# A new order for the work items of a recurrent-attention kernel, with three small moves in its feed-forward part and its head

## The chip, the cores and the metric

One core of one Trainium2 chip runs the whole kernel. The metric is device time in microseconds (us) of one execution; for each kernel the median of several runs is compared. The core has five engines with an instruction queue each: TensorE for matmuls (PE in the profile, PEld for its weight loads), VectorE (DVE), ScalarE (ACT), GpSimd (POOL), and SyncE (SP), which in this kernel only issues DMAs. The 16 DMA engines of the core move data between device memory (dram tensors) and the on-chip memory (`arena` in the profile). Matmul results land in eight banks of `ps`. An engine works through its own queue in order; waits on semaphores tie the queues together.

## The reference

The output is `g * a + (1 - g) * b` with three parts computed from the same x (2048 tokens of 640 values), all in bf16.

```python
def _A_ref(x, mem0, Wq, Wk, Wv, Wo, seg_len):      # 64 segments of 32 tokens, 32 heads of 192
    mem = mem0                                     # 8 rows
    for s in range(n_seg):
        h = concatenate([mem, x[s*32:(s+1)*32]])   # 40 rows of 640
        q, k, v = h @ Wq, h @ Wk, h @ Wv           # per head
        p = softmax(where(mask, q @ k.T * Dh**-0.5, -1e9))
        o = (p @ v) @ Wo
        mem = o[:8]; outs.append(o[8:])
    return concatenate(outs)
def _B_ref(x, w_gate, w_up, w_down):               # 640 -> 1536 -> 640
    return (gelu(x @ w_gate) * (x @ w_up)) @ w_down
g = sigmoid((x * gate_w).sum(-1, keepdims=True))
return g * a + (1 - g) * b
```

The mask of the reference is `(idx[:, None] < M) | (idx[:, None] >= idx[None, :])`. What matters for the time is the recurrence: the first eight rows of a segment's result are the memory of the next segment, so the 64 segments run one after the other. The projections of the 32 tokens that are no memory do not depend on it.

## The kernel before, in words

**Queues and dependencies.** The kernel writes one list of operations. A small scheduler class (`_Sched`) puts each operation at the end of its engine's queue, in the order in which the Python code emits it, and works out from the memory regions that it reads and writes which semaphores it waits for. Nothing is reordered later. Of several waits of a PE operation some are put onto the last matmuls of the operation before it. SP's queue is in program order too.

**Stages.** First the feed-forward part B for all tokens, in four blocks of 512 tokens: five transposed tiles of x (`ffn_transposes`, L818, on DVE), then for each of 12 tiles f the matmuls G (L828) and U (L831, five matmuls each), the gelu on ACT (L834) and the product h on DVE (L836); then `ffn_down`, which for each of four groups a of 128 tokens sums 12 tiles f, two matmuls a tile (512 and 128 columns: L850, L853). A few warming matmuls (L811) stand ahead. The result goes to a dram tensor, `ffn_b_scratch`.

Then come the four "left units" (L919), ahead of segment 0. The kernel calls "left" the tokens of a segment that it gathers over a group of four segments, because the eight-row memory and 24 of the 32 tokens fill a matmul's 32 rows, and eight tokens a segment are left over: eight tokens of four segments make another set of 32 rows. A left unit projects Q and K of one octet (one of four sets of eight heads) for such a group: matmuls, rows copied by ACT (L924), transposed by DVE (L926), stored to `left_qk_scratch`, from which a segment loads what it needs. Left V is projected apart (`vl_mm`, then `vl_evac`, which copies the bank on DVE or ACT).

Then come the 64 segments. `segment(s)` walks a list written out by hand, `PROGS[s % 4]`: the list `PROG` for s % 4 of 0, 1 and 2 and the list `PROG3` for 3. Each item makes the operations of one piece of work at the place where it stands in the list:

- `g n k`: piece k (of five along the 640) of the projections of group n; `GROUPS` gives which of Q, K, V (0, 1, 2) of which octet are in the group (L1119, or L226 where the rows in PE's weights are kept from the matmul before). With the last k, ACT empties the banks (rows L1140; V L1143). In a segment with s % 4 of 0, the V groups also project left V.
- `tq i`, `tk i`: DVE transposes the rows of Q or K of octet i (L1154); POOL makes a padded copy for Q (L1157).
- `sc i`: the scores of an octet: the mask first (L1165), then eight and more small matmuls (L1173, L234, L1180); DVE takes the maximum and subtracts (L1192, L1194).
- `ex i`: the softmax: ACT (L1204), then four operations on DVE (L1206 to L1211).
- `pt i`: transposes of the probabilities on PE (L1227, L1232), emptied by ACT (L1245).
- `pv i`: probabilities times V (L1260, L1262), emptied by ACT (L1278).
- `wo i h`: half an octet of the last product with Wo (L1296; the last octet L1321; with s % 4 of 3 L1339 for both token sets at once).
- `lf q u k`: only with s % 4 equal to q: piece k of a left unit for a later group (eight matmuls). `le q u m`: its row copy (L924), transpose (L926) and store; for `le 1 0` the two stores go out through SP (L1374), for the others one store through ACT's queue.
- `vb k`: only with s % 4 of 3: piece k of left V for the next group.

The octets are walked 0 to 3 in even and 3 to 0 in odd segments. The weights do not all fit on the chip: octets 0 and 3 share their slots for 13 of 15 projection pieces (384 KB each) and for three Wo pieces (480 KB each). After an item has read such a slot, SP loads the other octet's piece into it (`load_piece`, L628), so that each segment loads its missing pieces while it runs. The first three Wo pieces to be used give up their slots after `wo 0 0` (two) and `wo 0 1` (one), and the three pieces that come in, W13, W14 and W15 in the order of their use, are needed by `wo 3 0` and `wo 3 1`, the last items. SP's queue also holds the loads of x (L736), of left Q and K (L970) and of B's rows (L982, L988) and the stores of the result (L993, L1036).

At the end of a segment the sums of Wo are taken from the banks and transposed (`Tm`, L1517) into the memory rows of the next segment's h, which its first projections wait for.

Of the kernel before, what the change touches and what calls it, by code (L numbers as in the profile page):

```python
# [3 lines left out]
ACTF = mybir.ActivationFunctionType  # L4
# [234 lines left out]
def _build(nc, A_x, A_mem0, A_Wq, A_Wk, A_Wv, A_Wo, seg_len, w_gate, w_up, w_down,  # L239
# [277 lines left out]
    def piece_view(key, o):  # L517
        if key[0] == 3:
# [4 lines left out]
    PROG = [("g", 0, 0), ("g", 0, 1), ("g", 0, 2), ("g", 0, 3), ("g", 0, 4), ("tq", 0), ("g", 1, 0), ("g", 1, 1),  # L523
# [12 lines left out]
    PROG3 = [("g", 0, 0), ("g", 0, 1), ("g", 0, 2), ("g", 0, 3), ("g", 0, 4), ("g", 1, 0), ("tq", 0), ("tk", 0),  # L536
# [56 lines left out]
    o = 0  # L593
# [503 lines left out]
    def proj(s, item):  # L1097
        ms = GROUPS[item[1]]
        k = item[2]
        if k == 0:  # L1100
            for mi in ms:
                bk_of[mi] = LB if s % 4 == 0 and item[1] == 2 and mi[0] == 0 else misc_bank(s, item[1])
                if mi[0] == 2 and s % 4 == 0 and (s == 0 or mi[1]):
                    bk_of[(3, mi[1])] = OB if mi[1] == 1 else LB
# [504 lines left out]
```

## Time and profile before

| what | us |
|---|---|
| median of 3 runs | 1730.37 |
| lowest and highest run | 1717.53, 1730.9 |
| profiled execution | 1724.01 |
| its span (first to last instruction) | 1722.3 |
| PE busy | 1587.5 (92%) |
| DVE busy | 1003.5 (58%) |
| ACT busy | 776.6 (45%) |
| POOL busy | 548.6 (32%) |

The span holds some 171 us of feed-forward work, then six us of left units, then the segments at some 24 us each. The profile is of one execution. In its rows, `out<-in` names the tiles that an instruction writes and reads, `L1119` is a line of the kernel, `x8` a count. A timeline row has start, length, engine, line, operation, shapes and count, and in brackets the idle time of that engine just before and what ended it. A row of waits has the waiting and the awaited work, then microseconds in total, times, and the longest. "issue" is idle time for which no semaphore is found. SPq is the issuing of DMAs by SP.

### The profile page before, as it was taken

How to read it: one execution, taken by the hardware profiler on the slowest of the kernel's cores; microseconds unless marked ns; L12 is line 12 of the kernel's file. 1: busy time of each engine (PE TensorE's matmuls, PEld its weight loads, DVE VectorE, ACT ScalarE, POOL GpSimd, SP SyncE). 2: the span in 40 equal slices, each digit the busy share in tenths (PEclk: the TensorE clock that was granted, in tenths of full speed). 3: DMA queues.
4: the chain of work that ended last, by engine and by line, in shares of the span. 5: the costliest groups of instructions: out<-in, count | busy, mean ns of one | idle time of the engine just before them, and what ended most of it. 6: DMA issues, size and time to landing. Idle time of an engine off the chain costs nothing.

```text
span 1722.3 us, 75547 instructions
## 1 busy us (share of the span) xinstructions
PE 1587.5 (92%) x37107; PEld 778.1 (45%) x28147; DVE 1003.5 (58%) x2976; ACT 776.6 (45%) x1825; POOL 548.6 (32%) x1609
## 2 busy tenths in 40 slices
PE   9999899999999999999999899999999999999986
PEld 4444345444444444454444444454544444444443
DVE  5552666566565665655656656566665656555653
ACT  2222454545454454445444444445444544445442
POOL 1100233233333233333333333333333332333332
PEclk9999999999999999999999999999999999999998
DMA  9915988988888898879888898888888888988884
GB/s 298 326 37 153 342 311 296 322 308 297 297 299 319 307 323 281 305 276 329 295 287 302 294 333 281 283 288 319 310 298 288 296 316 289 310 280 303 314 313 170
DMA packets 278102, 499.27 MB, mean 290 GB/s; under 512 B 113951, under 2 KB 139015, under 8 KB 277767
## 3 DMA queue, kind: packets, MB, share of 16 engines
q1 hardware_dynamic: 249928, 482.45, 81.0%
q10 hardware_dynamic: 27839, 11.99, 2.5%
q8 instruction: 255, 4.18, 1.0%
q14 instruction: 80, 0.66, 0.1%
HBM read 473.25 MB, written 21.09 MB: 287 GB/s over the span
## 4 chain that ended last, share of the span: by engine, by line
PE 73%; DMA 12%; DVE 6%; ACT 4%; issue 3%; POOL 1%; SPq 0%; POOLq 0%; DVEq 0%; ACTq 0%
PE ps L1119 20%; PE ps L226 18%; DMA arena<-in_A_Wo_dram 6%; PE ps L1339 6%; PE ps L1296 5%; PE ps L1260 3%; PE ps L831 3%; PE ps L828 3%; PE ps L1165 3%; DMA arena<-in_A_Wv_dram 3%; PE ps L850 2%; PE ps L919 2%; PE ps L1173 1%; DMA arena<-in_A_Wk_dram 1%; ACT arena L1143 1%
## 5 line engine op out<-in xcount | busy, mean ns | idle before, releaser
L1119 PE MATMUL ps<-arena 128*32 128x384 bf16 x8660 | 650.9, 329 | 57.7 <-DVE arena L1517 47.4
L226 PE MATMUL ps<-arena 128*32 128x384 bf16 x8960 | 651.4, 326 | 7.7 <-DVE arena L1086 1.1
L1119 PEld LDWEIGHTS ps<-arena 128*32 128x32 bf16 x8660 | 221.7, 96 | 422.2 <-issue 265.6
L1154 DVE STREAM_TRANSPOSE arena<-arena 128x384 bf16<-128x384 bf16 x512 | 274.6, 561 | 125.8 <-ACT arena L1140 124.8
L1140 ACT ACTIVATE arena<-ps 128x384 bf16<-128x384 f32 x512 | 230.3, 493 | 233.8 <-PE ps L1119 223.3
L1296 PE MATMUL ps<-arena 128*32 128x320 bf16 x3456 | 187.1, 299 | 14.7 <-issue 13.4
L1157 POOL COPY arena<-arena 64x160 bf16<-64x160 bf16 x256 | 81.3, 318 | 374.3 <-DVE arena L1154 366.7
L1278 ACT ACTIVATE arena<-ps 128x480 bf16<-128x480 f32 (+1 forms) x256 | 137.6, 537 | 119.3 <-PE ps L1262 116.4
L1192 DVE TENSOR_REDUCE arena<-ps 104x4 f32<-104x160 f32 x256 | 82.9, 324 | 162.7 <-PE ps L1180 162.7
L1143 ACT ACTIVATE arena<-ps 128x384 bf16<-128x384 f32 x256 | 124.8, 488 | 106.9 <-PE ps L1119 105.3
L1245 ACT ACTIVATE arena<-ps 128x448 bf16<-128x448 f32 x192 | 104.6, 545 | 125.8 <-PE ps L1232 125.8
L1204 ACT ACTIVATE ps<-ps 104x160 f32<-104x160 f32 x256 | 75.8, 296 | 139.0 <-DVE ps L1194 137.1
L1206 DVE TENSOR_REDUCE arena<-ps 104x4 f32<-104x160 f32 x256 | 82.4, 322 | 95.7 <-ACT ps L1204 94.6
L976 POOL COPY arena<-arena 128x96 bf16<-128x96 bf16 x256 | 71.4, 279 | 201.2 <-PE ps L1180 163.8
L1296 PEld LDWEIGHTS ps<-arena 128*32 128x32 bf16 x3456 | 97.4, 96 | 68.2 <-issue 26.2
L1339 PE MATMUL ps<-arena 128*64 128x320 bf16 x1536 | 124.6, 305 | 1.2 <-ACT arena L1278 0.9
L1286 POOL COPY arena<-arena 128x96 bf16<-128x96 bf16 x192 | 51.3, 267 | 228.8 <-ACT arena L1278 222.6
L1260 PE MATMUL ps<-arena 128*64 128x160 bf16 x1536 | 118.3, 240 | 3.4 <-issue 3.3
L919 PE MATMUL ps<-arena 128*32 128x384 bf16 x1280 | 110.4, 328 | 0.0
L1262 PE MATMUL ps<-arena 128*64 128x64 bf16 x1536 | 104.2, 193 | 1.6 <-issue 1.3
L1260 PEld LDWEIGHTS ps<-arena 128*64 128x64 bf16 x1536 | 81.5, 109 | 47.5 <-ACT arena L1143 19.7
L1339 PEld LDWEIGHTS ps<-arena 128*64 128x64 bf16 x1536 | 79.9, 111 | 34.2 <-issue 10.4
(100 smaller groups left out, 2320.6 us busy)
## 6 DMA issues: line engine op xcount, KB each, us to landing
arena<-in_A_Wk_dram SPq DMA_DIRECT2D x335, 384.0 KB, 6.6
arena<-in_A_Wv_dram SPq DMA_DIRECT2D x335, 384.0 KB, 8.6
arena<-in_A_Wo_dram SPq DMA_DIRECT2D x205, 480.0 KB, 5.6
arena<-in_A_Wq_dram SPq DMA_DIRECT2D x209, 384.0 KB, 5.0
arena<-left_qk_scratch SPq DMA_DIRECT2D x126, 96.0 KB, 5.0
left_qk_scratch<-arena ACTq DMA_DIRECT2D x45, 192.0 KB, 4.1
left_qk_scratch<-arena SPq DMA_DIRECT2D x30, 96.0 KB, 4.5
ffn_b_scratch<-arena ACTq DMA_DIRECT2D x16, 160.0 KB, 3.1
```

The lines of the kernel that those rows point to most:

```text
L226: return e.add_instruction(mybir.InstMatmult(name=nm, start_tensor_calc=like["start"], stop_tensor_calc=stop, tile_size=(128, 32), tile_po ...
L919: fns.append(lambda e, outp=outp, rhs=rhs, j=j: e.matmul(outp, lhs, rhs, start=(k == 0), stop=(k == KT - 1), tile_position=(0, 32 * j)))
L1119: fns.append(lambda e, outp=outp, rhs=rhs, j=j: e.matmul(outp, lhs, rhs, start=(k == 0), stop=(k == KT - 1), tile_position=(0, 32 * j)))
L1140: S_.add("act", lambda e, m=m, bk=bk: e.activation(out=rows_sb[m], in_=ps[:, bk, 0:384], func=ACTF.Copy), reads=[r_ps[bk]], writes=[r_rows ...
L1143: S_.add("act", lambda e, i=i, bk=bk: e.activation(out=v_sb[i % NVB].rearrange("p (c n) -> p c n", c=3), in_=ps[:, bk, 0:384].rearrange("p ...
L1154: S_.add("dve", lambda e: e.transpose(out=dst[:, :, 0:L], in_=rows_sb[m].rearrange("p (c r) -> p c r", r=L)), reads=[r_rows[m]], writes=[r ...
L1245: S_.add("act", lambda e: e.activation(out=PT, in_=ps[:, bank, 0:PTW + 128], func=ACTF.Copy), reads=[r_ps[bank]], writes=[r_PT], name="pT ...
L1260: return [lambda e: e.matmul(full, v[:, e0:e0 + 64], PTm[:, i], start=True, stop=False, tile_position=(0, 64 * i), skip_group_check=True), ...
L1262: lambda e: e.matmul(part, vl[:, e0:e0 + 64], PTl[:, i], start=False, stop=True, tile_position=(0, 64 * i), skip_group_check=True)]
L1278: S_.add("act", lambda e: e.activation(out=apx(u[:, 0, 0, :], [[rs, na], [3 * rs, 4], [1, R]]), in_=ps[:, A, 0:na * W].rearrange("p (c t r ...
L1296: fns.append(lambda e, i=i, t=t, j=j, gv=gv: e.matmul(ps[32 * j:32 * j + 32, bank, 0:2 * DJ].rearrange("p (h n) -> p h n", h=2), lhs2[i], ...
L1339: S_.add("pe", [lambda e, i=i, g_=g_, c=c, p=p: e.matmul(ps[64 * i:64 * i + 64, LB, 0:2 * DJ], U3[:, p % 4, c, :], g_[:, c, 2 * DJ * i:2 * ...
```

## The change

Four edits, made together:

- **a.** `PROG` and `PROG3` get a new order. They hold the same items. Among the moves in `PROG`: `tk 0` stands ahead of `tq 0`; `sc 0` stands behind the last piece of group 1; `le 1 0` moves ahead of `wo 0 0`, with `ex 2` between its two halves; `wo 0 0` moves behind `g 4 3`, `g 4 4` and `g 5 0`; `wo 0 1` moves behind `g 5 2` and `sc 3`; `pv 2` no longer follows `sc 3` directly; `lf 1 1 3` moves from ahead of `wo 0 1` to behind `pv 3`.
- **b.** The first G tile of the first feed-forward block is made as five operations of one matmul, each of which reads one transposed tile of x.
- **c.** In `ffn_down`, for the first group a, the 22 matmuls of the first 11 tiles of h become an operation of their own; the last two matmuls are an operation that reads all of h, as before.
- **d.** Left V of the first octet of segment 0 is projected right behind the third of the four left units and emptied by ACT; before, its pieces stood among the pieces of segment 0's second V group, and DVE emptied them. The two functions for it are defined further up.

```diff
-    PROG = [("g", 0, 0), ("g", 0, 1), ("g", 0, 2), ("g", 0, 3), ("g", 0, 4), ("tq", 0), ("g", 1, 0), ("g", 1, 1),
-            ("tk", 0), ("g", 1, 2), ("sc", 0), ("g", 1, 3), ("ex", 0), ("g", 1, 4), ("g", 2, 0), ("g", 2, 1),
-            ("g", 2, 2), ("lf", 1, 0, 0), ("pt", 0), ("tq", 1), ("tk", 1), ("sc", 1), ("g", 2, 3), ("g", 2, 4),
-            ("tq", 2), ("ex", 1), ("lf", 2, 1, 0), ("lf", 1, 0, 1), ("lf", 1, 0, 2), ("pv", 0), ("g", 3, 0),
-            ("tk", 2), ("g", 3, 1), ("g", 3, 2), ("g", 3, 3), ("pt", 1), ("lf", 2, 1, 1), ("g", 3, 4), ("sc", 2),
-            ("ex", 2), ("lf", 2, 1, 2), ("pv", 1), ("g", 4, 0), ("g", 4, 1), ("lf", 0, 1, 0), ("g", 4, 2),
-            ("lf", 1, 0, 3), ("lf", 1, 0, 4), ("lf", 1, 1, 0), ("lf", 2, 1, 3), ("lf", 1, 1, 1), ("le", 1, 0, 0),
-            ("wo", 0, 0), ("tq", 3), ("g", 4, 3), ("le", 1, 0, 1), ("g", 4, 4), ("g", 5, 0), ("g", 5, 1),
-            ("lf", 1, 1, 2), ("lf", 0, 1, 1), ("pt", 2), ("lf", 1, 1, 3), ("wo", 0, 1), ("tk", 3), ("sc", 3),
-            ("pv", 2), ("g", 5, 2), ("wo", 1, 0), ("ex", 3), ("g", 5, 3), ("wo", 1, 1), ("g", 5, 4), ("wo", 2, 0),
-            ("pt", 3), ("lf", 0, 1, 2), ("wo", 2, 1), ("pv", 3), ("lf", 1, 1, 4), ("lf", 0, 1, 3), ("lf", 0, 1, 4),
-            ("le", 0, 1, 0), ("lf", 2, 1, 4), ("le", 2, 1, 0), ("le", 0, 1, 1), ("le", 1, 1, 0), ("le", 1, 1, 1),
-            ("wo", 3, 0), ("le", 2, 1, 1), ("wo", 3, 1)]
+    PROG = [("g", 0, 0), ("g", 0, 1), ("g", 0, 2), ("lf", 2, 1, 0), ("g", 0, 3), ("g", 0, 4), ("g", 1, 0), ("tk", 0),
+            ("g", 1, 1), ("tq", 0), ("g", 1, 2), ("g", 1, 3), ("g", 1, 4), ("sc", 0), ("g", 2, 0), ("lf", 2, 1, 1),
+            ("tq", 1), ("g", 2, 1), ("tk", 1), ("g", 2, 2), ("g", 2, 3), ("ex", 0), ("g", 2, 4), ("sc", 1),
+            ("pt", 0), ("ex", 1), ("tq", 2), ("g", 3, 0), ("g", 3, 1), ("g", 3, 2), ("pv", 0), ("lf", 1, 0, 0),
+            ("lf", 1, 0, 1), ("tk", 2), ("g", 3, 3), ("lf", 2, 1, 2), ("pt", 1), ("lf", 2, 1, 3), ("lf", 0, 1, 0),
+            ("g", 3, 4), ("lf", 1, 0, 2), ("sc", 2), ("pv", 1), ("lf", 1, 0, 3), ("lf", 1, 0, 4), ("lf", 0, 1, 1),
+            ("g", 4, 0), ("g", 4, 1), ("lf", 2, 1, 4), ("tq", 3), ("le", 1, 0, 0), ("ex", 2), ("g", 4, 2),
+            ("le", 1, 0, 1), ("lf", 1, 1, 0), ("g", 4, 3), ("g", 4, 4), ("lf", 1, 1, 1), ("g", 5, 0), ("wo", 0, 0),
+            ("tk", 3), ("g", 5, 1), ("pt", 2), ("lf", 1, 1, 2), ("g", 5, 2), ("sc", 3), ("lf", 0, 1, 2),
+            ("wo", 0, 1), ("wo", 1, 0), ("ex", 3), ("pv", 2), ("g", 5, 3), ("g", 5, 4), ("wo", 1, 1), ("pt", 3),
+            ("wo", 2, 0), ("wo", 2, 1), ("pv", 3), ("le", 2, 1, 0), ("lf", 1, 1, 3), ("lf", 0, 1, 3),
+            ("lf", 0, 1, 4), ("lf", 1, 1, 4), ("le", 1, 1, 0), ("le", 1, 1, 1), ("wo", 3, 0), ("le", 0, 1, 0),
+            ("le", 0, 1, 1), ("le", 2, 1, 1), ("wo", 3, 1)]
-    PROG3 = [("g", 0, 0), ("g", 0, 1), ("g", 0, 2), ("g", 0, 3), ("g", 0, 4), ("g", 1, 0), ("tq", 0), ("tk", 0),
...
+    PROG3 = [("g", 0, 0), ("g", 0, 1), ("g", 0, 2), ("g", 0, 3), ("g", 0, 4), ("g", 1, 0), ("g", 1, 1), ("g", 1, 2),
+            ("tk", 0), ("tq", 0), ("g", 1, 3), ("g", 1, 4), ("g", 2, 0), ("sc", 0), ("g", 2, 1), ("tq", 1),
...
+            ("wo", 1, 0), ("ex", 3), ("wo", 1, 1), ("pv", 2), ("g", 5, 1), ("g", 5, 2), ("g", 5, 3), ("pt", 3),
+            ("wo", 2, 0), ("g", 5, 4), ("wo", 2, 1), ("pv", 3), ("vb", 0), ("wo", 3, 0), ("wo", 3, 1), ("vb", 1),
+            ("vb", 2), ("vb", 3), ("vb", 4)]
...
-            S_.add("pe", [lambda e, k=k, f=f, gb=gb: e.matmul(...) for k in range(KT)],
-                   reads=[r_wg[NH * f // FT]] + r_xT, writes=[r_ps[gb]], name="ffn G %d %d" % (blk, f))
+            for ks in [(k,) for k in range(KT)] if blk + f == 0 else [tuple(range(KT))]:
+                S_.add("pe", [lambda e, k=k, f=f, gb=gb: e.matmul(...) for k in ks],
+                       reads=[r_wg[NH * f // FT]] + [r_xT[k] for k in ks], writes=[r_ps[gb]], name="ffn G %d %d" % (blk, f))
...
+                if a == 0 and f == FT - 1:
+                    S_.add("pe", fns, reads=[r_wd] + r_hT[:f], writes=wr, name="ffn down %d %d" % (blk, a))
+                    fns = []
...
+        if n == 2:
+            lb["v"] = 1
+            for k in range(KT):
+                vl_mm(0, k)
+            vl_evac(0, octet(0, 0), lb.pop("v"), "act")
...
-                if mi[0] == 2 and s % 4 == 0 and (s == 0 or mi[1]):
+                if mi[0] == 2 and s % 4 == 0 and mi[1]:
...
-            if m == 2 and s % 4 == 0 and (s == 0 or i):
+            if m == 2 and s % 4 == 0 and i:
...
-            if s % 4 == 0 and (s == 0 or i):
+            if s % 4 == 0 and i:
```

More of the change, by code (lines that the diff above doesn't have):

```diff
@@ L944, in unit_piece, with vl_evac, vl_mm @@
         return piece_view(key, res_off[key]), r_res[key]
+    def vl_evac(s, o, bk, eng="dve"):
+        out, in_ = vl_sb[o].rearrange("p (c n) -> p c n", c=3), ps[:, bk, 0:384].rearrange("p (n c) -> p c n", c=3)
+        if eng == "act":
+            S_.add("act", lambda e: e.activation(out=out, in_=in_, func=ACTF.Copy),
+                   reads=[r_ps[bk]], writes=[r_vl[o]], name="Vl evac s%d o%d" % (s, o))
+        else:
+            S_.add("dve", lambda e: e.tensor_copy(out=out, in_=in_),
+                   reads=[r_ps[bk]], writes=[r_vl[o]], name="Vl evac s%d o%d" % (s, o))
+    def vl_mm(s, k):
+        o, bk, b = octet(s, 0), lb["v"], s // 4 % 2
+        g_, rg_ = unit_piece((2, o, k))
+        S_.add("pe", [lambda e, j=j: e.matmul(
+            ps[32 * j:32 * j + 32, bk, 0:384], XLg[b][:, k, :], g_[:, 384 * j:384 * (j + 1)], start=(k == 0), stop=(k == KT - 1),
+            tile_position=(0, 32 * j)) for j in range(4)],
+            reads=[rg_, r_XLg[b]], writes=[r_ps[bk]], name="Vl s%d o%d k%d" % (s, o, k))
     units = [(0, NOCT - 1)] + [(1, o) for o in LUNIT[3].values()] + [(0, 1), (0, 2), (0, 0)]
```

21 lines of the change are left out of this document (3 added, 18 removed), and 12 rows, old and new, of the table PROG3.

## The prediction

> **What bounds the kernel now.** I read the page's totals first, then what PE waits for, then the windows of one group of four segments (56 to 59, one of each residue of s modulo 4; I call them q0 to q3).
>
> ```profile
> span 1722.3 us, 75547 instructions
> PE 1587.5 (92%) x37107; PEld 778.1 (45%) x28147; DVE 1003.5 (58%) x2976; ACT 776.6 (45%) x1825; POOL 548.6 (32%) x1609
> ...
> q8 instruction: 255, 4.18, 1.0%
> ```
>
> PE is busy 92% of the span. No line of this diff removes work from PE, so only its 1722.3 - 1587.5 = 135 us of gaps can be won, and the weights that are loaded anew in every segment can take some back. (The third row, the instruction queue, is for rival 1.) What the gaps wait for:
>
> ```profile
> PE ps L1119 <- DVE arena L1517: 47.4, 63, 1.1
> PE ps L1296 <- issue: 13.4, 18, 1.5
> PE ps L1321 <- DMA arena<-in_A_Wo_dram: 11.6, 20, 1.6
> ...
> PE ps L1173 <- DVE arena L1154: 6.6, 20, 0.5
> PE ps L1321 <- issue: 6.5, 10, 1.5
> PE ps L1119 <- ACT arena L1140: 5.4, 16, 0.9
> ...
> PE ps L850 <- DVE arena L836: 3.3, 4, 0.9
> ```
>
> Each row gives the sum, the number of times and the longest. The largest, 47.4 us, is the turn from one segment to the next (the new mem rows are transposed, L1517, before any projection); both lists end with the same Wo pieces and the turn behind them is not edited, so I leave it. The wait for Wo is a load: the last Wo piece (I call it W15), which the last item of a segment needs, isn't there yet. The rows by segment:
>
> ```profile
> 1518.73:1543.37 24.64, 22.27 (x613) 11.39 (x473) 16.45 (x50) 11.55 (x28) 7.60 (x25) 1.00 0.77 271
> 1543.37:1567.59 24.22, 22.32 (x593) 10.46 (x433) 14.97 (x46) 12.23 (x29) 8.27 (x25) 1.00 0.90 305
> 1567.59:1590.62 23.03, 21.14 (x554) 9.70 (x414) 13.77 (x44) 11.31 (x27) 7.80 (x24) 1.00 0.92 314
> 1590.62:1614.30 23.68, 22.95 (x509) 11.93 (x390) 12.22 (x41) 10.95 (x27) 9.36 (x27) 1.00 0.87 313
> ```
>
> The columns are window, length, PE, PEld, DVE, ACT, POOL, clock, DMA share, GB/s. The group takes 95.57 us. In q1 and q2 the DMA engines are busy at 0.90 and 0.92, and both end on W15:
>
> ```profile
> 1566.56 0.39 PE L1321 MATMUL ps<-arena 128*32 128x160 bf16 x12 [0.76 <-DMA arena<-in_A_Wo_dram]
> ...
> 1589.48 0.39 PE L1321 MATMUL ps<-arena 128*32 128x160 bf16 x12 [0.56 <-DMA arena<-in_A_Wo_dram]
> ```
>
> So in q1 and q2 a PE stall that goes is only waited for again at the end, unless W15 comes earlier. What matters there is when SP issues W13 to W15, and that hangs on items `wo 0 0` and `wo 0 1`, whose octet gives up the slots. The three loads beside their neighbours in SP's queue:
>
> ```profile
> 1528.39 5.00 SPq L1036 DMA_DIRECT2D out_dram<-arena  x8
> 1533.44 2.53 SPq L628 DMA_DIRECT2D arena<-in_A_Wo_dram  x3
> ...
> 1557.79 0.38 SPq L1374 DMA_DIRECT2D left_qk_scratch<-arena  x1
> 1558.22 1.00 SPq L628 DMA_DIRECT2D arena<-in_A_Wo_dram  x2
> 1559.26 0.43 SPq L1374 DMA_DIRECT2D left_qk_scratch<-arena  x1
> 1559.88 0.46 SPq L628 DMA_DIRECT2D arena<-in_A_Wo_dram  x1
> ...
> 1581.77 2.00 SPq L628 DMA_DIRECT2D arena<-in_A_Wo_dram  x3
> ```
>
> These are q0, q1 and q2. In q1 W15 issues at 1559.88 and PE gets it at 1566.56, 6.7 us later; in q2 the last of the three goes out about 1583.5 and is there at 1589.48, 6.0 us later.
>
> **FFN, parts b and c.**
>
> ```profile
> 5.68 3.25 DVE L818 STREAM_TRANSPOSE arena<-arena 128x512 bf16<-128x512 bf16 x5 [3.14 <-DMA arena<-in_A_x_dram]
> ...
> 9.08 1.69 PE L828 MATMUL ps<-arena 128*128 128x512 bf16 x5 [2.07 <-DVE arena L818]
> 10.56 2.34 PE L831 MATMUL ps<-arena 128*128 128x512 bf16 x5
> 15.08 1.24 PE L828 MATMUL ps<-arena 128*128 128x512 bf16 x5
> 9.00:12.70 3.70, 3.62 (x11) 1.37 (x12) 0.00 (x0) 0.60 (x1) 2.89 (x5) 0.60 1.10 326
> 37.68 0.39 PE L850 MATMUL ps<-arena 128*128 128x512 bf16 x1 [0.56 <-DVE arena L836]
> ```
>
> Down waits for the last h in each of the four blocks, 3.3 us in four. The other eleven tiles are 22 matmuls, eleven of them of 512 columns, which at a fifth of the 1.24 us of the row at 15.08 are 2.7 us alone, while the last h is less than 1 us away. All of it goes: **-3.3 us**. The next thing late is nothing: the extra op carries the same matmuls into the same two banks.
>
> G of the first tile waits 2.07 us for five transposes, which finish one each 0.65 us (3.25 / 5) from 6.33 to 8.93. With a wait of its own for each, four matmuls are done by 8.93, the fifth starts near 9.0 and U near 9.35 in place of 10.56: 1.2 us, if the weights of tile 0 had come by about 7.5 (the trace names only the DVE as what came last; if they came at 8.9, the gain is some 0.8). Five matmuls take 1.24 us at 15.08 and 2.34 at 10.56, and the clock granted in that stretch was 0.60. If the matmuls between 7 and 9 keep the clock up, U saves another 2.34 - 1.24 = 1.1 and G some 0.3. The Trainium skill, "TensorE: Matmul & The Clock Gate", Part 1, has the clock halved only after a window of about 3.4 us counted idle, which free-running windows make a matter of phase; by it the clock would stay and the gain be 2.6, by the rows alone 1.2. I take **-2.0**, ends -0.8 and -2.6.
>
> **Left V of segment 0, part d.**
>
> ```profile
> 184.08 0.49 PE L226 MATMUL ps<-arena 128*32 128x384 bf16 x8 [1.05 <-DVE arena L1086]
> ```
>
> The 20 matmuls (four for each of five k) move ahead of segment 0: no work less, and the wait of 1.05 us on its evacuation goes. But the evacuation is now one more on ACT (its size unpriced here; the 0.58 us that DVE takes to transpose such a tile, row 1558.40 below, bounds it) between left units 2 and 3, whose rows ACT also evacuates, and segment 0 ends, as q1 and q2 do, on its Wo loads. Ends: -1.05 and +0.6; I take **+0.3**, nearer to the second, since a stall taken out of a segment that ends on a load is not won.
>
> **The order, q0.** The same items, so the same PE work.
>
> ```profile
> 1524.32 0.51 PE L1119 MATMUL ps<-arena 128*32 128x384 bf16 x8 [0.31 <-ACT arena L1140]
> ...
> 1541.21 1.09 PE L1321 MATMUL ps<-arena 128*32 128x160 bf16 x48
> 1543.37 0.35 PE L1119 MATMUL ps<-arena 128*32 128x384 bf16 x4 [1.07 <-DVE arena L1517]
> arena<-in_A_Wo_dram SPq DMA_DIRECT2D x3, 480.0 KB, 4.4
> ```
>
> The left V of octet 1 waits for a bank that ACT has yet to empty, 5.4 us in 16 times: once in each q0. In the new list three more items stand between; this goes, 0.34 a time. Is there room before W15? It goes out near 1535.6, and by the 4.4 us that the three Wo loads of this segment take at the median it is in at 1540.0, 1.2 before the 48 matmuls that run at 1541.21 without a wait. Without a wait means a room of 0 at least; I take the middle, 0.6. The new list puts `wo 0 0` behind three more projection items and one left item (four matmuls take 0.35 and eight 0.51 by the rows at 1543.37 and 1524.32, so four more cost 0.16 and the eight of a left item 0.32), 0.80 in all, less the 0.34 that go; but W13 goes out right behind eight stores on SP as it is, so it moves by 0.5 at most, and the room covers that. Taken: -0.34 x 16 = **-5.4 us**, ends -7 (with the smaller stalls around it) and 0 (without room).
>
> **q1.** Here DVE and SP matter:
>
> ```profile
> 1556.16 0.32 DVE L1206 TENSOR_REDUCE arena<-ps 104x4 f32<-104x160 f32 x1 [0.35 <-ACT ps L1204]
> 1556.94 0.18 DVE L1211 TENSOR_TENSOR arena<-ps,arena 104x32 bf16<-104x32 f32 x1
> 1558.40 0.58 DVE L926 STREAM_TRANSPOSE arena<-arena 128x384 bf16<-128x384 bf16 x1 [0.18 <-ACT arena L924]
> ```
>
> The softmax of octet 2 (`ex 2`, DVE from 1556.16 to 1557.12, 0.96 us) stood ahead of both transposes of `le 1 0`; the new list has it between them. And both stores of `le 1 0` now stand ahead of W13 and W14 on SP, where the old list had W13 and W14 between them. The second store can't go before its transpose (1558.40 + 0.58 = 1558.98), so W13, out at 1558.22 before, would go out behind 1559.26 + 0.43 = 1559.7, 1.5 us later, if `le 1 0` stayed where it was; by PE's order `wo 0 0` comes only 0.5 later (three projection items). I take 0.9 between the two, W14 some 0.6 and W15, which stood behind the second store already, 0.2. Who waits for SP: the three loads alone. They are 1440 KB, 4.7 us at q1's 305 GB/s, and 1559.88 + 4.7 = 1564.6 is ahead of the 1566.5 at which W15 came, so part of the delay is caught up. I take W15 0.3 later: **+0.3 x 16 = +4.8 us**, ends 0 and +0.9 (W13's delay whole). The transposes on DVE are also 0.96 later for K of octet 3 and so for `sc 3`, whose wait was 6.6 us in 20; but the 0.76 us wait on W15 behind it takes that in.
>
> **q2.** The list puts `wo 0 0` 0.80 later, as in q0. The DMA engines are busy at 0.92 over this window, so the bytes, not the issue, should set the landing: +0.1, ends 0 and +1.0 (rival 2): **+1.6 us**. **q3** waits little for Wo; scores moved behind `g 2 0`, and the four `vb` items moved behind `wo 3 1`, are covered by its 22.95 us of PE in 23.68: **-0.5**.
>
> **The sum.** -3.3 - 2.0 + 0.3 - 5.4 + 4.8 + 1.6 - 0.5 = -4.5. The profiled execution took 1724.0 us in all (the span and 1.7 around it), so 1719.5. The median shown is 1730.4 and the lowest 1717.5: the profiled one lies between, 6.4 under the median. I say 1720; this is 0.6% under the median and inside what the three runs differ by, so about 1% is what a measurement tells from no change.
>
> **Rivals.** For the second I need the price of `sc 3`:
>
> ```profile
> 1559.77 0.25 PE L1165 MATMUL ps<-arena 128*40 128x160 bf16 x2
> 1560.22 0.28 PE L1173 MATMUL ps<-arena 128*40 128x40 bf16 x8 [0.20 <-DVE arena L1154]
> ...
> 1560.44 0.24 PE L1260 MATMUL ps<-arena 128*64 128x160 bf16 x2
> ```
>
> Rival 1, more is won: the PE stalls that go, go whole, and instruction blocks happen to be crossed elsewhere. The rows named issue are 13.4 + 6.5 = 20 us in 28 times, and PE's 37,107 matmuls and 28,147 weight loads over the 255 packets of the instruction queue are 256 to a packet: a gap of 0.7 us at about every ninth block. The new order moves the places; if half fall where PE waits for W15 anyway, 10 us go: 1719.5 - 10 = 1709.5. For it: q1 and q2 have such waits; against: other gaps can come. The Trainium skill, "Runtime: NRT & Kernel Launch", Instruction fetch mechanics, calls a crossing "mostly hidden"; 28 gaps at 255 packets agree with mostly, and the 20 us say that the rest isn't nothing.
>
> Rival 2, slower: **W15's time after its issue is fixed** (6.0 us in q2, 6.7 in q1), so that each piece of PE work which the list takes from behind `wo 0 1` shows at the end. From behind it go, in q0 and q2, `sc 3` (0.47 us: 1559.77 to 1560.44 less the wait of 0.20), `g 5 2` (0.16) and one left item (0.32), 0.95 in all; in q1 the first two go and a left item comes, 0.31. In q0 W15 goes out 0.95 - 0.34 = 0.61 later against a room of 0.6: nothing; q1 pays 0.31 + 0.2 for the store, q2 0.95: 1.46, or 1.5, x 16 = +24, FFN, head and q3 -5.5: 1742. It decides once the engines are drained when W15 goes out. For it: q0, with 0.77 overall, has idle engines somewhere; against: q1 and q2, where the price falls due, are at 0.90 and 0.92.
>
> Rival 3, the list does nothing: only the FFN's 5 us stay, 1719, which no one number tells from the forecast.
>
> **Chances.** Forecast with rival 3, 0.48; rival 1, 0.25; rival 2, 0.23; other, 0.04. The median lies some 6 us from the lowest and the profiled time, so 6 is the scatter that I add. The range goes from 1701 (rival 1 less 2 for q0's far end and 6 of scatter) to 1748 (rival 2 and the scatter). Faster by over 1% (under 1713): most of rival 1 and a little of the forecast's own scatter, 0.27. Slower by over 1% (over 1747.7): the upper part of rival 2, 0.16. Within: 0.57.
>
> **What would show it.** PE's waits: L850 behind L836 gone, L828 behind L818 below 0.7, L1119 behind L1140 under 1 us. W15's issue in q1 at 16.7 us after the segment's start (16.5 now, 1559.88 - 1543.37), and L1321 behind the Wo load 15 to 20 us in sum in place of 11.6. Group period 95.2 to 95.6. Wrong if q2's windows grow by over 0.4 (rival 2), or if the rows named issue change by 10 us.

## The result, and the profile after

The changed kernel is slower: 1750.35 us median (1738.31 to 1758.44, six runs) against 1729.2 us of the kernel before in the same runs (1717.53 to 1730.93, six runs), a ratio of 1.0148 with a 95% interval of 1.0117 to 1.0179. Run again beside other kernels it gave 1.0148 again. The forecast was 1720.

The profiled execution took 1738.3 us. Its page, totals:

```profile
span 1736.6 us, 75669 instructions
PE 1579.4 (91%) x37090; PEld 765.9 (44%) x28147; DVE 986.8 (57%) x2975; ACT 788.4 (45%) x1826; POOL 550.1 (32%) x1609
```

**The small moves did in this execution what was forecast.** The feed-forward part, in PE's timeline after (start, length, line, count, idle time ahead and what ended it):

```profile
7.98 1.25 PE L829 MATMUL ps<-arena 128*128 128x512 bf16 x5 [0.86 <-DMA arena<-in_B_w_gate_dram]
9.51 1.25 PE L832 MATMUL ps<-arena 128*128 128x512 bf16 x5 [0.28 <-DMA arena<-in_B_w_up_dram]
10.60 1.24 PE L829 MATMUL ps<-arena 128*128 128x512 bf16 x5
...
34.73 0.39 PE L855 MATMUL ps<-arena 128*128 128x512 bf16 x1
```

G (L829 now) waits for its weights and no longer for the transposes, the five U matmuls take 1.25 us in place of 2.34, and down (L855) starts at 34.73 with no wait, where it was 37.68. Segment 1 starts 4.6 us earlier; the two rows are of before and after:

```profile
205.88 0.35 PE L1119 MATMUL ps<-arena 128*32 128x384 bf16 x4 [0.64 <-DVE arena L1517]
```

```profile
201.29 0.35 PE L1128 MATMUL ps<-arena 128*32 128x384 bf16 x4 [0.64 <-DVE arena L1526]
```

So the loss is in the segments: 14.3 us of the profiled execution and the 4.6 that had been won, some 19 us. What PE waits for there, by the waits of after:

```profile
PE ps L1128 <- DVE arena L1526: 41.5, 63, 1.1
PE ps L1330 <- DMA arena<-in_A_Wo_dram: 37.2, 41, 2.3
PE ps L1330 <- ACT arena L1287: 9.2, 16, 0.6
...
PE ps L962 <- ACT arena L1287: 3.6, 14, 0.3
...
PE ps L1128 <- ACT arena L1149: 2.7, 1, 2.7
```

L1330 is the last octet's Wo (L1321 before). Its wait for the loads went from 11.6 us in 20 to 37.2 in 41, and a wait for ACT has come up, 9.2 us in 16, 14 of them in segments with s % 4 of 2: `wo 3 0` waits for ACT to empty `pv 3` (1.7 us in three before), because `lf 2 1 4` no longer stands between the two. In segments with s % 4 of 3 the left V (L962) now waits for ACT, 0.26 us a time. The wait of the left V for a bank (5.4 us in 16) is gone but for one, at the head. The windows of segments 56 to 59 show where this falls:

```profile
1531.67:1556.75 25.08, 22.42 (x612) 11.24 (x472) 16.43 (x50) 11.92 (x28) 7.99 (x25) 1.00 0.77 265
1556.75:1581.14 24.39, 21.81 (x593) 9.99 (x433) 14.60 (x46) 12.36 (x29) 8.23 (x25) 1.00 0.91 309
1581.14:1604.53 23.39, 20.64 (x553) 9.36 (x414) 13.44 (x44) 11.44 (x27) 7.99 (x24) 0.99 0.90 307
1604.53:1629.00 24.47, 23.88 (x509) 12.15 (x389) 12.05 (x41) 10.98 (x27) 9.43 (x26) 0.94 0.85 300
```

The column to read is the third from the right, the clock: 0.94 in the last segment, which had 1.00 before. Look at the end of segment 58 in slices of 3.41 us, the length in which the clock changes in this trace. After:

```profile
1597.14:1600.55 3.41, 3.41 (x100) 2.20 (x88) 1.66 (x7) 2.02 (x5) 1.26 (x3) 1.00 0.97 340
1600.55:1603.97 3.42, 1.39 (x50) 0.81 (x48) 1.96 (x6) 1.39 (x4) 2.28 (x6) 1.00 0.60 178
1603.97:1607.38 3.41, 2.85 (x36) 0.75 (x20) 1.17 (x5) 0.00 (x0) 1.03 (x4) 0.50 0.90 258
1607.38:1610.80 3.42, 3.42 (x94) 0.85 (x40) 1.04 (x2) 1.79 (x5) 0.32 (x1) 1.00 0.81 259
```

and the same place before:

```profile
1586.69:1590.10 3.41, 2.50 (x69) 1.46 (x65) 2.05 (x6) 1.74 (x4) 2.02 (x6) 1.00 0.55 197
1590.10:1593.52 3.42, 2.90 (x72) 0.85 (x32) 1.75 (x7) 0.87 (x2) 1.57 (x5) 1.00 0.89 207
```

After, PE is busy 1.39 of 3.42 us, 41%, and the next slice runs at a clock of 0.50: 36 matmuls in 2.85 us where 94 fit into 3.42. Before, PE was busy 73% in the slice at the end of the segment, and the clock stayed at 1.00. PE's timeline after shows the three waits, of which the first two and the start of the third fall into the slice, and the slow matmuls behind them (the first row names L1390, the copy that ACT makes right behind emptying `pv 3`):

```profile
1601.48 1.10 PE L1330 MATMUL ps<-arena 128*32 128x160 bf16 x36 [0.92 <-ACT arena L1390]
1603.40 0.39 PE L1330 MATMUL ps<-arena 128*32 128x160 bf16 x12 [0.82 <-DMA arena<-in_A_Wo_dram]
1604.53 0.51 PE L1128 MATMUL ps<-arena 128*32 128x384 bf16 x4 [0.74 <-DVE arena L1526]
1604.82 0.54 PE L226 MATMUL ps<-arena 128*32 128x384 bf16 x4
```

Four such matmuls take 0.54 us, and 0.34 at the full clock. I call such a stretch of 3.41 us a slow slice. Between 206 and 1700 us the profile before has one; the profile after has 12 (two of them two slices long, counted once here and below), 11 of them at the end of a segment with s % 4 of 1 or 2 or at the start of the one behind it. A second profile of the changed kernel has 12 as well. Segments that no slow slice touches are in sum as long as before: over segments 1 to 62 the means of the four kinds add up to 95.35 us after, 95.37 in the second profile and 95.24 before. By kind (s % 4 of 0, 1, 2, 3) they differ by -0.07, +0.20, +0.23 and -0.25 us in the first profile, and by +0.26, -0.03, -0.05 and -0.05 in the second. The segments that a slow slice touches are together 18.9 us longer than such a mean (21.3 in the second profile, 1.2 before). That is the loss of the profiled execution. The half clock itself can make at most 1.7 us of a slice, 24 us for these 14; the rest of an excess is the waits that bring it on.

The page's sums alone would be read otherwise. PE's gaps rose by 22 us (1722.3 - 1587.5 = 134.8, 1736.6 - 1579.4 = 157.2) and its busy time fell by 8.1 with the same matmuls, half clock included. The matmul rows lie closer together after: the 3456 rows of 299 ns of `wo` (L1296, L1305) cover 187.1 us before and 152.0 after. So part of what PE waited before stood inside its busy time, and the 22 us are not the price of the new waits.

From here on q0 to q3 are again the segments by s % 4. The clock theory is then: the list puts more waits into the last 3 us of q1 and q2, and what costs is not their length but the half clock that follows. Its rival is the prediction's second: W15 lands later, and its wait is the loss.

### The profile page after: what moved, and what is told of

It is laid out like the page before. It is cut to its first block, busy times and chain, and to the rows that moved or that the text cites. A ratio compares the mean times of both kernels' runs of the same rounds, so it can differ in the third digit from the quotient of the medians.

```text
span 1736.6 us, 75669 instructions
## 1 busy us (share of the span) xinstructions
PE 1579.4 (91%) x37090; PEld 765.9 (44%) x28147; DVE 986.8 (57%) x2975; ACT 788.4 (45%) x1826; POOL 550.1 (32%) x1609
## 4 chain that ended last, share of the span: by engine, by line
PE 69%; DMA 16%; SPq 4%; DVE 4%; issue 3%; ACT 2%; POOL 1%; DVEq 0%; POOLq 0%; ACTq 0%
PE ps L1128 20%; PE ps L226 19%; DMA arena<-in_A_Wo_dram 10%; PE ps L1348 6%; DMA arena<-in_A_Wv_dram 5%; PE ps L1305 4%; PE ps L1269 3%; PE ps L923 3%; PE ps L1174 2%; PE ps L829 1%; PE ps L832 1%; PE ps L1182 1%; SPq L628 1%; PE ps L855 1%; PE ps L234 1%
## 5 line engine op out<-in xcount | busy, mean ns | idle before, releaser
L1128 PEld LDWEIGHTS ps<-arena 128*32 128x32 bf16 x8640 | 223.2, 98 | 455.7 <-issue 302.0
L1201 DVE TENSOR_REDUCE arena<-ps 104x4 f32<-104x160 f32 x256 | 82.7, 323 | 186.1 <-PE ps L1189 186.1
L1305 PE MATMUL ps<-arena 128*32 128x320 bf16 x3456 | 152.0, 299 | 1.6 <-issue 1.5
L1330 PE MATMUL ps<-arena 128*32 128x160 bf16 x2304 | 64.6, 236 | 54.9 <-DMA arena<-in_A_Wo_dram 37.2
L1215 DVE TENSOR_REDUCE arena<-ps 104x4 f32<-104x160 f32 x256 | 79.1, 309 | 55.5 <-ACT ps L1213 53.8
L1269 PEld LDWEIGHTS ps<-arena 128*64 128x64 bf16 x1536 | 81.4, 109 | 58.1 <-issue 24.5
L1305 PEld LDWEIGHTS ps<-arena 128*32 128x32 bf16 x3456 | 91.1, 96 | 30.6 <-issue 3.5
```

The costliest lines, as they stand in the source:

```text
L1128: fns.append(lambda e, outp=outp, rhs=rhs, j=j: e.matmul(outp, lhs, rhs, start=(k == 0), stop=(k == KT - 1), tile_position=(0, 32 * j)))
L1269: return [lambda e: e.matmul(full, v[:, e0:e0 + 64], PTm[:, i], start=True, stop=False, tile_position=(0, 64 * i), skip_group_check=True), ...
L1305: fns.append(lambda e, i=i, t=t, j=j, gv=gv: e.matmul(ps[32 * j:32 * j + 32, bank, 0:2 * DJ].rearrange("p (h n) -> p h n", h=2), lhs2[i], ...
```

## The experiments

Each result is a ratio to the kernel before, measured beside it, with its 95% interval; the clock is the mean over the runs, 0.992 for before.

**The parts alone.** The first kernel has the old lists with parts b, c and d, the second the new lists alone.

```diff
 small moves:  PROG, PROG3 as before; parts b, c, d
 lists:        PROG, PROG3 as after; the rest as before
```

> Kernel before with parts b, c and d alone; both lists as they were. The theories do not part here, the run gives the size of the small moves: segment 1 starts 4.6 us earlier in the profile of the changed kernel (201.3 in place of 205.9), so about 1725 by the median (ratio 0.997), with the clock at half in no more than one or two windows between 206 and 1700 us, as before.

> Kernel before with the two new lists alone. Both theories: slower than the changed kernel by the 4.6 us of the small moves, ratio about 1.017, some 12 windows of half clock. If the ratio is under 1.010, the loss needs list and small moves together.

Small moves alone: 0.9988 (0.9955 to 1.002), clock 0.993. Lists alone: 1.0159 (1.0117 to 1.0202), clock 0.979, 12 slow slices. The list makes the whole loss. The small moves won less than the 4.6 us: in their profile segment 1 starts at 204.45, 1.4 us earlier than before, and down has a new wait for DVE to empty a bank of two groups earlier, which the early start brings on:

```profile
PE ps L855 <- DVE arena L865: 3.1, 1, 3.1
```

**Filling the waits.** Useless matmuls, in the changed kernel and in the one with the small moves alone:

```diff
+    def fill(s, n):   # n matmuls of 512 columns on the identity, into a bank that no one holds
+        S_.add("pe", [...] * n, reads=[r_ident], writes=[r_ps[bk]])
...
+            if p == allp[-1] and s % 4 in (1, 2):   # ahead of the last Wo piece
+                fill(s, 2)
...
+        fill(s, 3)                                  # behind the last Wo matmul of a segment
```

> The changed kernel with useless matmuls added (0.22 us each, into a bank that is free): three behind each segment's last Wo matmul, two ahead of the last Wo piece where s % 4 is 1 or 2, two behind pv 3 where it is 2. Nothing that loads or orders the rest is touched. Clock theory (the waits of the new list pile up in one window of 3.41 us, PE is busy under 45% of it, and the clock is at half for the next 3.41 us; that is the whole loss of the list): at most 3 windows of half clock between 206 and 1700 us in place of 12, ratio 0.995 to 1.003. Load theory (the loss is that W15 lands later): the fill wins nothing, ratio 1.013 to 1.020.

> Kernel before with parts b, c, d and with the same fill behind the last Wo matmul (three) and ahead of the last Wo piece (two). Clock theory: before had one window of half clock in the profiled run and its slower runs may have more, so this is the fill's gain on the old lists: 1 to 8 us under the run with the small moves alone, ratio 0.992 to 0.997. Load theory: like the small moves alone or some 3 us slower by the fill, 0.997 to 1.000.

The changed kernel with fill (it has two more behind `pv 3` in q2): 1.0035 (1.0009 to 1.006), clock 0.995, one slow slice. The old lists with fill: 1.0035 (1.0019 to 1.0051), clock 0.996. So the first moved as the clock theory says, just over its range, and with the fill in both the new lists cost nothing against the old ones. But I was wrong on the second: the fill itself costs some 8 us (1.0035 against 0.9988) where the clock had little to give. A smaller fill, only in q1 and q2 and not ahead of the last Wo piece, cost less:

```diff
-        fill(s, 3)
+        if q in (1, 2):
+            fill(s, 2)
...
+                if i == NOCT - 1 and q == 2:   # behind pv 3
+                    fill(s, 2)
```

> The changed kernel with a smaller fill, only in segments with s % 4 of 1 and 2: two useless matmuls behind the last Wo matmul and, where it is 2, two behind pv 3; none ahead of the last Wo piece, none in the other segments, where the fill of the earlier run cost time. Clock theory: at most 4 slow windows, and with the fill's cost down from 8 to about 2 us, ratio 0.999 to 1.003. Load theory: 1.013 to 1.017.

1.0001 (0.9968 to 1.0034), clock 0.992, with six slow slices in the profile, two more than expected. The changed kernel with 96 more matmuls is 1.5% faster than without. The waits for the loads are what they are without fill. This kernel, and then the second profile of the changed kernel:

```profile
PE ps L1330 <- DMA arena<-in_A_Wo_dram: 29.0, 40, 1.7
```

```profile
PE ps L1330 <- DMA arena<-in_A_Wo_dram: 29.4, 34, 1.7
```

The sum differs by 8 us between two profiles of the changed kernel (37.2 and 29.4), so 29.0 is no gain. A theory by which these waits are the loss doesn't allow that.

**The same fill, thin.** To separate what the matmuls do to the clock from what four more instructions do at that place:

```diff
-        e.matmul(ps[:, bk, 0:512]..., ident, ident.broadcast..., start=True, stop=True)
+        e.matmul(ps[:, bk, 0:8], ident, ident[:, 0:8], start=True, stop=True)
```

> As the smaller fill that brought the changed kernel back to 1.0001, with the same instructions at the same places and with the same dependencies, but each useless matmul has 8 columns in place of 512, so PE is hardly busier. Clock theory: the slow windows stay, clock about 0.980 to 0.983, ratio 1.012 to 1.016. If the fill worked by its place in the queue (a wait that it takes over, another order of arrival): 0.998 to 1.003.

1.0057 (1.0028 to 1.0087), clock 0.983, nine slow slices in the profile. The clock did as expected, the time did not: it lies 0.9% under the changed kernel. Against the wide fill of the same instructions, 1.0001, the clock is worth 0.56%, some 10 us, give or take 8 by the two intervals. So much of the 25 us a pair of equal instruction counts shows. The rest of the thin fill's gain I looked for by place, with the changed kernel beside it:

```diff
 thin, one place each:
+    fill(s, 2)   # only behind pv 3 of q2
+    fill(s, 2)   # only behind the last Wo matmul of q1 and q2
```

> The changed kernel once more, beside the next three on one chip. Both: ratio 1.012 to 1.018, clock 0.978 to 0.983.

> The changed kernel with the two 8-column matmuls behind pv 3 where s % 4 is 2, and none at the turn. If the 0.9% that the thin fill won beside the clock comes from this place (it takes over one of the two waits of wo 3 0, which has no other PE work ahead of it in the new list): ratio 1.006 to 1.009. If not: 1.012 to 1.017.

> The changed kernel with the two 8-column matmuls at the turn where s % 4 is 1 or 2, and none behind pv 3. If the 0.9% comes from here (the last Wo operation is rid of two waits that stood in its tail): 1.006 to 1.009. If not: 1.012 to 1.017. If both places give nothing alone, the thin fill's gain stays unexplained.

The changed kernel: 1.0148 (1.0078 to 1.0219), clock 0.980. Thin behind `pv 3`: 1.0047 (1.0016 to 1.0078), clock 0.983. Thin at the turn: 1.0076 (1.004 to 1.0113), clock 0.981. Either place alone gives 0.7 to 1.0%, and both together no more. My two guesses on waits fall with that: they would add up.

In the profiles, gaps of PE with no wait inside q0 segments come to 19 us (24 in the second profile) in the changed kernel, to 10 and 8 in these two and to 14 with both. These are the gaps that the rows name issue, and they hang on the count of instructions ahead. To see this, count PE's matmuls and weight loads together: all 39 such gaps of the profile before stand at a count that leaves 194 when divided by 256, and 1.2 to 1.6 us behind the end of a packet of the instruction queue. They are the crossings of rival 1.

A group of four segments has 3969 of these records in the changed kernel, 15.5 blocks, so the crossings meet the same items in every second group; the thin fills make it 3972 to 3980, and they move on. q0 segments, which hold no fill, lost with that about what their gaps lost: 24.51 us in the mean in the changed kernel (24.85 in its second profile), 24.26 with both fills, 24.07 and 23.80 with one. That is 4 to 11 us over 16 segments against the first profile. It agrees with the thin fills' gain, but rests on one profile of each.

**Which segments.** The old list in q2 alone, then in q1 and q2:

```diff
-    PROGS = (PROG, PROG, PROG, PROG3)
+    PROGS = (NEW, NEW, PROG, NEW3)    # first kernel
+    PROGS = (NEW, PROG, PROG, NEW3)   # second kernel
```

> The changed kernel with the old list in the segments with s % 4 of 2 alone. Clock theory: 9 of the 12 slow windows of the changed kernel lie at the ends of these segments, so about 3 remain, excess in slow segments from 19 us to about 5; ratio 1.004 (1.0148 less 14 us of 1729, and q2's own 0.2 a segment). Load theory: what q2 lost goes (0.57 a segment x 16 = 9 us): 1.0095.

> The changed kernel with the old list where s % 4 is 1 and 2, the new one where it is 0 and 3. Clock theory: the slow windows followed on the ends of 1 and 2 alone, so at most 4 are left, clock 0.992; the segments 0 and 3 that no slow window touches were 0.07 and 0.25 us shorter with the new lists, 5 us in all: ratio 0.995 to 0.999 (the small moves alone gave 0.9988). If the new lists of 0 and 3 carry loss of their own: 1.002 or more.

First: 1.0046 (1.001 to 1.0082), clock 0.988. Second: 0.9977 (0.9947 to 1.0006), clock 0.993. Of the 1.7% between the changed kernel and the second, 1.0 comes from q2's list, the rest from q1's, and the new lists of q0 and q3 are harmless. The times came as the clock theory had them, the counts did not: the profiles have nine and five slow slices, where about three and at most four were expected. (The 9 of 12 in the first expectation are 8: one of the slices lies behind a q0.)

**Which items.** Two single moves back, and one in the other direction:

```diff
 lf back:       ..., ("pv", 3), ..., ("lf", 2, 1, 4), ("le", 2, 1, 0), ("wo", 3, 0), ...      # new list
 wo 0 1 early:  ..., ("lf", 1, 1, 2), ("wo", 0, 1), ("g", 5, 2), ("sc", 3), ("lf", 0, 1, 2), ...   # new list
 lf early:      ..., ("lf", 2, 1, 4), ("pt", 2), ("lf", 1, 1, 3), ("wo", 0, 1), ...                # old list
```

> The changed kernel with one item moved back: lf 2 1 4 (eight matmuls, 0.33 us, only in segments with s % 4 of 2) again between pv 3 and wo 3 0. Clock theory: PE's busy share in the last window of q2 goes from 0.41 to about 0.51, over the 0.46 under which the slow windows followed: at most 5 slow windows, ratio 1.005. Load theory: W13 to W15 go out 0.33 us earlier in q2 and the end comes 0.3 earlier at most: 5 us, ratio 1.012.

> The changed kernel with one item moved: wo 0 1 ahead of g 5 2, sc 3 and lf 0 1 2, so that W15 goes out some 0.6 us (q1) to 0.9 us earlier (q0). If the landing follows the issue (rival 2 of the prediction), W15 lands 0.5 earlier in q1 and q2 and the wait for it (37.2 us in 41) falls to under 20; then the slow windows go too, ratio 1.002. If the bytes set the landing (the forecast), the landing moves by under 0.2, 10 slow windows stay, ratio 1.012 to 1.015.

> The mirror of the run that moved lf 2 1 4 back: old lists with b, c and d, and lf 2 1 4 moved from behind pv 3 to ahead of pt 2 and wo 0 1, where the new list has it. Clock theory: q2's last window loses 0.33 us of PE work (0.10 of its busy share), slow windows go from 3 to 6 or more, clock 0.988, ratio 1.003 to 1.008. Load theory: W15 goes out 0.33 us later in q2, 5 us in all: 1.002, with the slow windows as before.

`lf 2 1 4` back: 1.0076 (1.0048 to 1.0104), clock 0.986. This one item of 0.33 us, which runs in 16 of 64 segments, is worth 0.7%, some 12 us: more than twice the PE time that it shifts (5 us), so it works by more than its length. The slow slices fell to 10 in the profile, not to 5. In its waits that of `wo 3 0` for ACT is gone and that for Wo nearly as long as after:

```profile
PE ps L1318 <- DMA arena<-in_A_Wo_dram: 32.3, 39, 2.2
```

`wo 0 1` early: 1.0129 (1.0063 to 1.0195), clock 0.982, 13 slow slices: no gain. In q0, W15 went out 16.90 us after the segment's start in place of 18.05 and landed at 22.54 in place of 22.66: 1.15 earlier out, 0.12 earlier in. In q0 the landing does not follow the issue. But the edit did not do what the expectation says of q1 and q2, where the price falls due: W15 went out there at 17.24 and 16.73 in place of 17.41 and 16.79, so the run says nothing of them. They are answered by before and after, in the next section. (The gaps named issue came to 39 us, against 27 and 34 in the two profiles of the changed kernel, so the ratio may be up to 0.7% worse than the move deserves.)

The mirror in the old list: 1.0004 (0.9973 to 1.0035), clock 0.989, seven slow slices in place of three. The wait is made as in the changed kernel:

```profile
PE ps L1318 <- ACT arena L1275: 9.0, 16, 0.6
```

The clock fell as expected; the time rose by 0.16% against the small moves alone, within the intervals, where the fall of the clock, 0.004, would be 8 us by the line below. The run does not prove the price of the wait.

**A version that beats both?** Old lists in 1 and 2, new ones in 0 and 3, with the two matmuls at the turn of q1 and q2, thin and wide; and the old lists with the two wide ones at the turn of q0 to q2:

```diff
+    PROGS = (NEW, PROG, PROG, NEW3)
+        if q in (1, 2):
+            fill(s, 2)   # 8 columns in the first, 512 in the second
```

> Old lists, parts b, c and d, and two useless matmuls of 512 columns behind the last Wo matmul of the segments with s % 4 of 0, 1 and 2. By the line through the runs without fill (1709 us and 20.7 us more for each 0.01 of clock lost) the small moves alone stand at a clock of 0.9926. Clock theory: clock 0.995, 5 us less than the small moves alone (0.9988), ratio 0.995 to 0.997, a version under both kernels. Otherwise 0.998 to 1.001.

> Old list where s % 4 is 1 and 2, new list where it is 0 and 3, parts b, c, d (0.9977 as it stood), and two 8-column matmuls at the turn of 1 and 2. In the changed kernel these four instructions a group of four segments took 10 us off beside the clock, and the gaps named issue inside segments with s % 4 of 0 went from 17 us to 7. If that is where instruction blocks are crossed, it depends on the count of instructions and can go either way here: 0.990 to 1.001, with the clock as before (0.992).

> The same with 512 columns: the same instructions, so the same places of the instruction blocks, and more PE work at the turn. Clock theory: clock 0.995 in place of 0.992, 6 us under the run with thin matmuls, less what the fill costs (the old lists with such a fill ended 9 us over the line through the runs without one): 3 us faster to 3 us slower than the thin one.

Old lists with the wide fill: 1.0018 (0.9998 to 1.0037), clock 0.995: the clock rose, and the fill cost more than that gave. Mixed lists: thin 1.0009 (0.9984 to 1.0034), clock 0.989 and not 0.992 as expected; wide 0.9964 (0.9938 to 0.999), clock 0.994, 1719.68 us median: 0.4% under the kernel before and 1.8% under the changed one. The pair has the same instructions in the same places, and the one that keeps PE busier is 7 us faster, more than the 3 that the expectation allowed. Its core's row in the profiled execution:

```profile
core 0: 1720.2 us, clock 0.993
```

and that of the changed kernel:

```profile
core 0: 1736.6 us, clock 0.982
```

**All runs on one line.** Time against the granted clock over 195 single runs, of before, the changed kernel (both sets) and the seven experiments without fill (0.01 of clock lost is 35 us at half clock, ten slow slices):

| kernel | median us | mean clock | above the line, us |
|---|---|---|---|
| before | 1725.0 | 0.992 | 0.8 |
| small moves | 1722.8 | 0.993 | -1.7 |
| new lists in q0, q3 | 1720.9 | 0.993 | -3.4 |
| old lists, lf early | 1725.1 | 0.989 | -4.6 |
| old list in q2 | 1732.2 | 0.988 | -1.7 |
| lf back | 1738.3 | 0.986 | 0.6 |
| wo 0 1 early | 1745.7 | 0.982 | 1.5 |
| changed kernel | 1750.4 | 0.980 | -0.3 |
| lists alone | 1756.4 | 0.979 | 2.4 |
| thin fill, both places | 1732.9 | 0.983 | -9.2 |
| wide fill, small | 1725.0 | 0.992 | -0.6 |

The line is 1709.0 us and 20.5 us for each 0.01 of clock lost, with a spread of 3.8 us around it. The last two rows are not part of the fit, and neither are the other fills: the thin ones at one place lie 10 us under the line, the mixed lists 4 us under it (thin) and on it (wide), the wide fills of the old lists 19 and 9 us over it and the large fill of the changed kernel 13. Between before and the changed kernel the clock differs by 0.0123, by the line 25 us; the medians differ by 25.4. Within the single kernels alone, where no edit comes in, 0.01 of clock goes with 20.8 us. A slow slice goes with 2 us, more than the 1.7 that half clock itself can cost, so it includes waits that bring it on.

## Why the prediction was wrong

The direction was wrong, and the time lay over the range, 1750 against 1701 to 1748. By its steps (means of segments are over 4 to 59 where nothing else is said):

- **The ceiling, 135 us of gaps.** Not one: with the same matmuls PE's busy time fell by 8.1 us. Busy is not work at full rate here.
- **FFN, -3.3 and -2.0.** Right up to the first down: down starts 2.95 us earlier at 34.73, of which 2.1 come from G, and G's gain came as the clock sentence had it: the slices there ran at 1.00. What bounded G was the weights, the condition that the text named. The other blocks' waits for h are gone too. But "the next thing late is nothing" was wrong: in the second block down waits 0.9 to 3.9 us for banks that DVE has yet to empty. In the 17 profiles with parts b and c the left units start 1.6 to 5.1 us earlier than before, 3.6 in the mean, against a forecast of 5.3. That the changed kernel's profile shows nearly 5 of them is luck of that execution.
- **Left V, +0.3.** Not measured alone. From the first left unit to segment 1 it takes 35.3 us after (165.94 to 201.29) and 35.1 before, with the new list in that stretch and a slow slice at 180.6 us. Its wait for ACT, 0.9 us before, is 2.7, which the step saw as a risk.
- **q0, -5.4.** The wait went, the gain did not come: q0 segments took 24.68 us in the mean after and 24.66 before, though W15's wait did not grow there. Gaps named issue inside q0 rose from 13 us to 19 (24 in the second profile), as much as the gain forecast. The room before W15, taken as 0.6, was 0.6 (in at 22.3 us, its first matmul at 22.9), but W15 took 5.2 us and not 4.4.
- **q1, +4.8, and q2, +1.6.** The signs were right; q1 came near, +0.25 a segment (4 us in 16), and q2 did not, +0.57 (9 us). The step on SP's queue was half right: both stores go ahead, and W13 goes out 0.6 us later (0.9 forecast), but W15 not later at all. In the profile of segment 57:

```profile
1570.45 1.70 SPq L1383 DMA_DIRECT2D left_qk_scratch<-arena  x2
1572.20 2.57 SPq L628 DMA_DIRECT2D arena<-in_A_Wo_dram  x3
```

  The three loads go out together from 1572.20, 15.45 us after the segment's start (14.85 before). PE gets W15 at 1580.11, 23.4 after the start, 23.2 before. In the mean W15 lands 0.5 us later in q1 and 0.6 to 0.7 in q2. Where no slow slice touches the segment it is less: 0.4 and 0.2 us in the one profile, 0.2 and 0.1 in the second, in q2 with an issue 0.7 to 0.8 later. The forecast had 0.3 and 0.1.
- **q3, -0.5.** Of the other sign: +0.30 a segment. Its new wait is that of left V, 0.26 us, and where no slow slice touches it q3 is 0.25 us shorter than before (0.05 in the second profile). It is longer because it starts at half clock behind q2.
- **The step that failed** is the one on which the terms for q1, q2 and q3 rest: each wait was priced at its length, and a stall that is "only waited for again at the end", where the wait on W15 "takes that in", at nothing. The row for Wo, forecast at 15 to 20 us, came to 37.2 (29.4 in the second profile), and what such a wait costs depends on what else falls into the same 3.41 us. Behind `pv 3`, ahead of W15 and at the turn together the waits leave PE busy 41% of a slice, and the clock is halved behind it: 12 times in place of once, and 18.9 us in the segments touched. Of the 25 us between the medians, the thin and the wide fill show 10 as the clock's; the clock that was lost can make 21 at most (0.0123 of 1738). How the rest divides between half clock and the waits that bring it on stays open. I had the mechanism in hand for the head of the kernel and did not ask for it at the 63 turns. I also left `lf 2 1 4` out, which is worth 0.7%.
- **Rival 2** came nearest in time, 1742, and its sign came too, since q2's windows grew by over 0.4. Its reason the runs speak against: in q0 a W15 that goes out 1.15 us earlier lands 0.12 earlier, and in q2 one that goes out 0.7 to 0.8 later lands 0.1 to 0.2 later, in segments without a slow slice. The forecast's view, that the bytes and not the issue set the landing, held there; what it forecast from that did not.
- **Rival 1** (instruction blocks) is real, 19 to 39 us in the profiles, and moved in all directions; it took q0's gain, and in the thin fills it is the likely reason for the 9 us beside the clock. The second part rests on the counts and on q0's lengths above; no run moves the crossings alone.

The Trainium skill, "TensorE: Matmul & The Clock Gate", "HAM oscillation — how this bites in real kernels", speaks of idle gaps over some 3.4 us as what halves the clock. Here no single wait at these turns is longer than 2.3 us, and it was halved all the same.

## What to carry to other kernels

Ahead of the price of a wait, sum PE's idle time over the slice of 3.4 us in which it falls: if PE is left under half busy there, add some 2 us for the matmuls that follow at half clock. Look at the clock column of every stage, also of those that are no warm-up, and compare the mean clocks of two kernels before you compare their waits. A reorder that fills early waits and leaves the late ones bare can lose though no single wait is long; a few useless matmuls in an idle slot that is certain are a cheap test of that.

## What the runs showed of the hardware

- How busy is busy enough. In six profiles without fill (before, changed twice, lists alone, small moves, old lists with `lf` early), cut into the 3.413 us slices in which the clock changes, slices at full clock between 206 and 1690 us: of 27 with PE busy under 0.43 of the time, 26 were followed by a slice at half clock; from 0.43 to 0.47, 11 of 15; from 0.47 to 0.56, 9 of 41; from 0.56 to 0.70, none of 139. Busy is the union of the matmul rows; their ends are modelled, so the bounds are rough.
- A gap of PE that the rows name issue is a crossing of a block of instructions: in the profile before all 39 stand a whole number of 256 matmuls and weight loads apart. 39 of some 255 crossings show, 25 us in all.
- The slices run on without regard to the segments, so the same program meets them otherwise in each run: the six runs of the changed kernel had clocks from 0.976 (1758.4 us) to 0.983 (1739.5 us). Much of the spread between runs of one kernel goes with it.
- Two matmuls of 8 columns do not hold the clock up (0.983 against 0.980), two of 512 in the same places do (0.992).
